# Float64 weights to float32: the low word added as an integer instead of multiplied and added as a float

## The chip, the core and the metric

The kernel runs on one core of a Trainium2 chip. The time is device microseconds (us) of one execution; lower is better. The engines named below are TensorE (PE; its weight loads are PEld), VectorE (DVE), ScalarE (ACT), GpSimd (POOL) and the queue that issues the transfers (SP). Each engine takes its own instructions strictly in the order in which they stand in its queue.

## What is computed

Causal attention over 4 batches of 8 heads with 576 tokens of 64 features, mixed with a linear-attention memory by a gate, gives 2304 rows of 512 numbers. These go through two gated feed-forward blocks:

```python
gate = 1.0 / (1.0 + np.exp(-(x @ w_gate)))     # 512 x 1536
val = x @ w_val                                # 512 x 1536
x = (gate * val @ w_out).astype(np.float32)    # 1536 x 512
h = x @ w_in                                   # 512 x 2048
g = h * np.clip(h + 3.0, 0.0, 6.0) / 6.0
return (g @ w_out).astype(np.float32)          # 2048 x 512
```

The five weight matrices arrive as float64. The kernel gets their bits as pairs of 32-bit words, a low and a high word for each number, makes float32 of them, and splits each float32 in an upper and a lower part for TensorE, so that every product is three matrix multiplications (upper by upper, upper by lower, lower by upper).

## The kernel before

Three phases share the engines. **Phase A** (to about 395 us) runs the attention, in 32 visits of one head pair and one half of its rows, and mixes into it the first half (6 of 12 column blocks of 128) of the first feed-forward block for the first 1872 tokens, in six chunks of 312 (`moe_a`). **Phase B** (to about 684 us) does the rest of the first block: 36 items of one token chunk and one column block each, `g1` (two products into `g`, then the tanh of line 673 on ACT, the multiplication of line 674 on DVE, and the split of the result `hs` on ACT and DVE) and, one item later, `g2` (the product of `hs` into `acc`). **Phase C** does the second block in three groups of 768 tokens, with seven products for the eight of a 2 by 2 block multiplication (`product`, line 787) and the product of the gated result into `acc` (line 822).

The weights of phases A and B and those of C are converted while A and B run. `w_load` fetches two tiles of 512 columns a time, as 128 x 512 pairs of words, into one of two buffers `wst`; `w_convert` turns the older buffer into float32 through `value`, which works in a scratch tile `wf` with a single buffer. In phase A one conversion takes both tiles at once (`self.wide` is 2: 9 conversions of 1024 columns); after that it takes one tile (`self.wide` is 1: 50 conversions of 512 columns, 18 for phase B and 32 for phase C). `convert` adds the upper part (ACT, line 163) and the lower part (DVE, line 164) and writes them to `wslot`; `convert_pair` does so for phase C, where 16 of the 32 tiles first go through four sums (lines 184 to 187) and are then split (lines 201 and 202), and stores the result in DRAM (`wd`).

In phase B a call of `w_next` (convert one pair of tiles, load the next) stands behind an item by the count in `goal`:

```python
goal = min(2 * i + 2, 4) + (max(i - 1, 0) * 2 * NPAIR + 26) // 27
while done < min(goal, 4 + 2 * NPAIR):
    self.w_next()
```

With NPAIR = 8 the last of the 20 calls is written behind the 28th of the 36 items. Behind the 31st and 32nd item stand `c_load(0)` and `c_sums()`: phase C's first input `xh` is loaded, its second half into a buffer `wst` once that is free, the other `wst` becomes `xt`, and POOL forms three sums in them (line 735). Behind the 32nd to 35th item stand 2, 2, 1 and 2 of the seven `c_block` calls, each of which splits one block of 768 columns (`xq`) on ACT and DVE (lines 228 and 229).

That is the order in which the code is written. On TensorE phases A and C keep it. Everywhere else a scheduler sets the order of each queue when the program is built, from its own estimate of every instruction's time: an instruction that it expects to be late is put behind others.

Of the kernel before, what the change touches and what calls it, by code (L numbers as in the profile page):

```python
# [8 lines left out]
F32 = mybir.dt.float32  # L9
F32R = mybir.dt.float32r  # L10
I32 = mybir.dt.int32
U32 = mybir.dt.uint32
AF = mybir.ActivationFunctionType
ALU = mybir.AluOpType
# [64 lines left out]
class Kernel:  # L79
# [64 lines left out]

    def value(self, st):

        nc = self.nc
        lo, hi = st[:, :, :, 0], st[:, :, :, 1]
        w = self.stage.tile([128, self.wide, 512], F32, name="wf", tag="wf", bufs=1)
        wi, hif, lof = w.bitcast(I32), hi.bitcast(F32), lo.bitcast(F32)  # L150
        nc.scalar.activation(w, hif, AF.Abs)
        nc.vector.tensor_scalar(w, w, HI_MIN, HI_MAX, op0=ALU.max, op1=ALU.min)
        nc.vector.tensor_scalar(wi, wi, 0x07FFFFFF, 3, op0=ALU.bitwise_and, op1=ALU.logical_shift_left)
        nc.vector.scalar_tensor_tensor(hi, hi, -0x40000000, wi, op0=ALU.bitwise_and, op1=ALU.bitwise_or)
        nc.vector.tensor_scalar(wi, hi, -0x800000, None, op0=ALU.bitwise_and)
        yield hif
        nc.vector.scalar_tensor_tensor(lof, lo.bitcast(U32), 2.0**-52, w, op0=ALU.mult, op1=ALU.mult)
        nc.vector.tensor_tensor(hif, hif, lof, op=ALU.add)

    def convert(self, sl, st):  # L160
        nc = self.nc
        for hif in self.value(st):
            nc.scalar.copy(sl[:, 0], hif)
        nc.vector.tensor_tensor(sl[:, 1], hif, sl[:, 0].bitcast(F32), op=ALU.subtract)

    def convert_pair(self, j, up, st):
# [807 lines left out]
```

## Time and profile before

| | |
|---|---|
| median of 3 runs | 1079.51 us (1079.44 to 1081.23) |
| the profiled execution | 1079.94 us |
| its span, first to last instruction | 1078.2 us |
| TensorE busy | 1037.6 us (96%), 5824 matmuls |
| VectorE busy | 684.2 us (63%), 1602 instructions |
| ScalarE busy | 551.5 us (51%), 1191 instructions |
| GpSimd busy | 83.2 us (8%), 102 instructions |
| 16 DMA engines busy | 44.5% of the span |

The profile is of one execution. A busy TensorE is not one at its peak, since matmuls overlap; what matters is where it has no matmul at all, and at which clock it works. The granted clock is a share of 2.4 GHz; 0.5 is 1.2 GHz, and a value between them is a mean over a stretch in which both occurred.

### The profile page before, as it was taken

To read this page: it belongs to the slowest core of one execution; us is meant where nothing else is said; L and a number is where in the kernel's file an instruction comes from. 1 tells how busy PE (TensorE), PEld (TensorE's weight loads), DVE (VectorE), ACT (ScalarE), POOL (GpSimd) and SP (SyncE) were. 2 spreads that over 40 slices of the span, in tenths; PEclk is the share of its full clock that TensorE was granted. 3 is DMA by queue.
4 is the path that set the end of the run, shared out by engine and by line. 5 is a ranking of instruction groups with operands and counts; after the bars stand their busy time and mean duration, and the time that the engine had idled before them with its cause. 6 is when DMAs were issued, how large, how long until landed. Compare 5 with 4: busy or idle time off the path is not lost.

```text
span 1078.2 us, 16086 instructions
## 1 busy us (share of the span) xinstructions
PE 1037.6 (96%) x5824; PEld 890.3 (83%) x5824; DVE 684.2 (63%) x1602; ACT 551.5 (51%) x1191; POOL 83.2 (8%) x102
## 2 busy tenths in 40 slices
PE   4789999999999999999999999799999999999998
PEld 2457768877887899999888888688888888888886
DVE  7999885454455348899898988854355333643432
ACT  5989885576556644435434433434344333543432
POOL 3212211110111000000000000320002000000000
PEclk9879999999999999999999999899999999999999
DMA  6645642424242225227586776645305543044511
GB/s 217 220 170 182 202 129 68 141 79 120 59 134 79 64 85 175 93 102 260 216 292 221 257 250 221 228 178 215 122 27 184 186 148 135 1 153 190 215 40 59
DMA packets 66239, 164.87 MB, mean 153 GB/s; under 512 B 8432, under 2 KB 41712, under 8 KB 60272
## 3 DMA queue, kind: packets, MB, share of 16 engines
q1 hardware_dynamic: 66160, 163.85, 44.5%
q8 instruction: 46, 0.75, 0.3%
q14 instruction: 33, 0.27, 0.1%
HBM read 122.76 MB, written 41.06 MB: 152 GB/s over the span
## 4 chain that ended last, share of the span: by engine, by line
PE 85%; DVE 7%; ACT 3%; DMA 2%; issue 1%; POOL 1%; SPq 0%; POOLq 0%; ACTq 0%
PE acc L822 18%; PE pa L787 9%; PE pb L787 7%; PE g L235 6%; PE g L233 6%; PE g L234 6%; PE m L233 5%; PE m L234 5%; PE m L235 5%; PE pv L426 4%; PE t L402 4%; PE s L344 3%; PE acc L233 3%; PE acc L235 3%; PE acc L234 3%; DMA aux<-in_aux 2%
## 5 line engine op out<-in xcount | busy, mean ns | idle before, releaser
L822 PE MATMUL acc<-wslot,hs 128*128 128x512 f32 x864 | 227.8, 395 | 2.2 <-ACT hs L228 2.2
L822 PEld LDWEIGHTS acc<-wslot,hs 128*128 128x128 f32 x864 | 159.5, 188 | 27.7 <-ACT hs L228 3.5
L787 PE MATMUL pa<-xq,wslot 128*128 128x384 f32 x576 | 119.3, 342 | 7.3 <-ACT xq L228 5.4
L787 PEld LDWEIGHTS pa<-xq,wslot 128*128 128x128 f32 x576 | 105.1, 190 | 16.6 <-ACT xq L228 5.8
L235 PE MATMUL g<-xs,wslot 128*128 128x468 f32 (+1 forms) x288 | 106.1, 369 | 0.0
L234 PE MATMUL g<-xs,wslot 128*128 128x468 f32 (+1 forms) x288 | 105.6, 369 | 0.0
L233 PE MATMUL g<-xs,wslot 128*128 128x468 f32 (+1 forms) x288 | 103.9, 369 | 0.0
L362 ACT ACTIVATE P<-P,m 128x192 f32<-128x192 f32 (+4 forms) x144 | 84.1, 586 | 31.2 <-DVE m L324 29.8
L233 PE MATMUL m<-xs,wslot 128*128 128x312 f32 x288 | 93.7, 325 | 0.0
L787 PE MATMUL pb<-xq,wslot 128*128 128x384 f32 x432 | 89.1, 341 | 0.2 <-DVE xq L229 0.2
L234 PE MATMUL m<-xs,wslot 128*128 128x312 f32 x288 | 88.1, 306 | 0.0
L235 PE MATMUL m<-xs,wslot 128*128 128x312 f32 x288 | 87.8, 305 | 0.0
L344 PE MATMUL s<-qk 64*128 64x320 f32 (+3 forms) x320 | 70.8, 502 | 14.3 <-DMA qk<-in_qk 11.8
L787 PEld LDWEIGHTS pb<-xq,wslot 128*128 128x128 f32 x432 | 78.6, 189 | 7.0 <-DVE xq L229 0.7
L851 DVE TENSOR_TENSOR c<-pb,u 128x384 f32<-128x384 f32 x48 | 26.6, 555 | 88.1 <-ACT u L887 87.1
L402 PEld LDWEIGHTS t<-ident,P 128*128 128x128 f32 x464 | 53.8, 145 | 27.2 <-issue 14.5
L799 ACT ACTIVATE r<-c,three 128x384 f32<-128x384 f32 x72 | 44.2, 614 | 61.9 <-DVE c L851 61.9
L402 PE MATMUL t<-ident,P 128*128 128x128 f32 x464 | 68.4, 285 | 7.5 <-POOL P L377 4.1
L229 DVE TENSOR_TENSOR hs<-r,hs 128x384 fp32r<-128x384 f32 x96 | 55.9, 586 | 26.3 <-ACT hs L228 24.8
L404 ACT COPY T<-t 128x512 f32<-128x512 f32 (+2 forms) x128 | 65.7, 540 | 12.1 <-PE t L402 11.9
L324 DVE CUSTOM_DVE_ANT_0 P<-s,mask 128x320 f32<-128x320 f32 (+3 forms) x144 | 62.5, 451 | 14.5 <-PE s L344 14.2
L426 PE MATMUL pv<-T,aux 128*64 128x256 f32 (+2 forms) x512 | 63.4, 377 | 4.5 <-ACT T L404 4.5
(102 smaller groups left out, 1966.9 us busy)
## 6 DMA issues: line engine op xcount, KB each, us to landing
wst<-in_wm SPq DMA_DIRECT2D x68, 512.0 KB, 5.7
wslot<-wd SPq DMA_DIRECT2D x30, 1024.0 KB, 5.0
wd<-wslot SPq DMA_DIRECT2D x16, 1024.0 KB, 4.4
wslot<-wd SPq DMA_DIRECT2D x15, 768.0 KB, 6.3
wd<-wslot SPq DMA_DIRECT2D x8, 768.0 KB, 5.8
qk<-in_qk SPq DMA_DIRECT2D x32, 160.0 KB, 2.3
aux<-in_aux SPq DMA_DIRECT2D x16, 320.0 KB, 3.3
qk<-in_qk SPq DMA_DIRECT2D x16, 288.0 KB, 3.0
```

The source lines that it names most:

```text
L229: elo.tensor_tensor(lo, src, hi.bitcast(F32), op=ALU.subtract)
L233: nc.tensor.matmul(out, w[0], x[0], start=first, stop=False)
L234: nc.tensor.matmul(out, w[0], x[1], start=False, stop=False)
L235: nc.tensor.matmul(out, w[1], x[0], start=False, stop=last)
L324: self.nc.vector.tensor_tensor_reduce(out=self.row(v, rg, r, 64 + a, 64 + e), in0=ps, in1=mask, scale=-0.125, scalar=3.0e38 if a == 0 else ...
L344: nc.tensor.matmul(ps[:, : e - a], qk[rows, 0, q0 : q0 + 128], qk[rows, 1, a:e], start=True, stop=True)
L362: self.nc.scalar.activation(x, x, AF.Exp, bias=vs["m", rg][:, r : r + 1], scale=-1.0, accum_out=vs["l", rg][:, r : r + 1])
L402: nc.tensor.transpose(ps[:, 128 * n : 128 * n + 128], self.row(v, rg, r, 128 * j, 128 * j + 128), self.ident)
L404: nc.scalar.copy(pr["T", rg][:, 512 * k : 512 * k + c], ps[:, :c])
L426: nc.tensor.matmul(ps[rows, o : o + w], pr["v"][:, j, rows], T[:, c : c + w], start=(n == 0), stop=(n == last), skip_group_check=True,)
L787: nc.tensor.matmul(ps[:, :HC], w[:, i, b, cc], x[:, l, k], start=first and k == 0 and n == 0, stop=last and k == 1 and n == 2, skip_group_ ...
L822: nc.tensor.matmul(a, h[:, i, cc], w[:, l, f], start=first and f == 0 and n == 0, stop=last and f == 1 and n == 2)
```

## The change

`value` keeps its first four steps: the absolute value of the high word read as a float (ACT), clamp, mask and shift, and the joining of sign and shifted bits (DVE). After these the high word holds a float32 whose last three bits are open; the low word's top bits belong there. Before, the exponent of that float was masked out into `wf` (line 155), the low word as an integer was multiplied with 2^-52 and that power of two (line 157), and the product was added as a float (line 158). Now the low word is scaled by 2^-29 and rounded to an integer, and the two words are added as integers: the last bits of the float are counted up. In conversions of one tile the scaling is done on ACT, into the low word's place, and the join goes to `wf`, from which `convert` takes the upper part; in conversions of two tiles the scaling is done on DVE into `wf`.

```diff
-        wi, hif, lof = w.bitcast(I32), hi.bitcast(F32), lo.bitcast(F32)
+        wi, hif = w.bitcast(I32), hi.bitcast(F32)
         nc.scalar.activation(w, hif, AF.Abs)
         nc.vector.tensor_scalar(w, w, HI_MIN, HI_MAX, op0=ALU.max, op1=ALU.min)
         nc.vector.tensor_scalar(wi, wi, 0x07FFFFFF, 3, op0=ALU.bitwise_and, op1=ALU.logical_shift_left)
+        if self.wide == 1:
+            nc.scalar.activation(lo, lo.bitcast(U32), AF.Copy, scale=2.0**-29)
+            nc.vector.scalar_tensor_tensor(wi, hi, -0x40000000, wi, op0=ALU.bitwise_and, op1=ALU.bitwise_or)
+            yield w
+            nc.vector.tensor_tensor(hi, wi, lo, op=ALU.add)
+            return
         nc.vector.scalar_tensor_tensor(hi, hi, -0x40000000, wi, op0=ALU.bitwise_and, op1=ALU.bitwise_or)
-        nc.vector.tensor_scalar(wi, hi, -0x800000, None, op0=ALU.bitwise_and)
         yield hif
-        nc.vector.scalar_tensor_tensor(lof, lo.bitcast(U32), 2.0**-52, w, op0=ALU.mult, op1=ALU.mult)
-        nc.vector.tensor_tensor(hif, hif, lof, op=ALU.add)
+        nc.vector.tensor_scalar(wi, lo.bitcast(U32), 2.0**-29, None, op0=ALU.mult)
+        nc.vector.tensor_tensor(hi, hi, wi, op=ALU.add)
...
-        for hif in self.value(st):
-            nc.scalar.copy(sl[:, 0], hif)
+        hif = st[:, :, :, 1].bitcast(F32)
+        for upper in self.value(st):
+            nc.scalar.copy(sl[:, 0], upper)
```

In the built program lines behind the change stand 7 lower: line 164 is now 171, 229 is 236, 674 is 681. The integer addition (line 159, or 164 for two tiles) becomes an instruction that the listing calls ISA, with 512 (1024) times 2 elements in a lane.

The scheduler builds other queues from it. At the end of phase B, VectorE's queue before, from the 36th and last item's line 674 on (`wst` and `wf` are the conversion, `hs` the item, `xp` phase B's output):

```order
L674 SCALAR_TENSOR_TENSOR th<-th,g 128x468
L152 TENSOR_SCALAR wf<-wf 128x512
L164 TENSOR_TENSOR wslot<-wst,wslot 128x512
L153 TENSOR_SCALAR wf<-wf 128x512
L229 TENSOR_TENSOR hs<-th,hs 128x468
L154 SCALAR_TENSOR_TENSOR wst<-wst,wf 128x512
L155 TENSOR_SCALAR wf<-wst 128x512
L157 SCALAR_TENSOR_TENSOR wst<-wst,wf 128x512
L158 TENSOR_TENSOR wst<-wst 128x512
L694 SCALAR_TENSOR_TENSOR xp<-acc,xp 128x468 x2
L164 TENSOR_TENSOR wslot<-wst,wslot 128x512
```

The last conversion stands behind the last item there. VectorE's queue now, from just ahead of the 32nd item's line 681 to just behind the 34th's:

```order
L157 SCALAR_TENSOR_TENSOR wf<-wst,wf 128x512
L681 SCALAR_TENSOR_TENSOR th<-th,g 128x468
L159 ISA wst<-wst,wf 128x512x2
L236 TENSOR_TENSOR xq<-xh,xq 128x768
L171 TENSOR_TENSOR wslot<-wst,wslot 128x512
L236 TENSOR_TENSOR hs<-th,hs 128x468
L681 SCALAR_TENSOR_TENSOR th<-th,g 128x468
L236 TENSOR_TENSOR xq<-xt,xq 128x768
L236 TENSOR_TENSOR hs<-th,hs 128x468
L236 TENSOR_TENSOR xq<-xh,xq 128x768
L681 SCALAR_TENSOR_TENSOR th<-th,g 128x468
L236 TENSOR_TENSOR xq<-xt,xq 128x768
```

The last conversion ends (line 171) between the 32nd and the 33rd item, and the splits of phase C's first blocks (`xq`), of which five stood behind the last item, all stand ahead of it.

ScalarE's queue in phase B before, from the 30th item's tanh on:

```order
L673 ACTIVATE th<-g 128x468
L228 CAST xs_6906<-x 128x468
L151 ACTIVATE wf<-wst 128x512
L228 CAST xs_6909<-x 128x468
L228 CAST xs_6912<-x 128x468
L228 CAST xs_6915<-x 128x468
L228 CAST hs<-th 128x468
L151 ACTIVATE wf<-wst 128x512
```

ScalarE's queue now at the same item (line 156 is the new scaling of the low word, 152 the absolute value):

```order
L680 ACTIVATE th<-g 128x468
L156 ACTIVATE wst<-wst 128x512
L235 CAST xs_6847<-x 128x468
L235 CAST xs_6850<-x 128x468
L235 CAST xs_6853<-x 128x468
L156 ACTIVATE wst<-wst 128x512
L152 ACTIVATE wf<-wst 128x512
L235 CAST xs_6856<-x 128x468
L235 CAST hs<-th 128x468
```

Two scalings now stand ahead of the cast of `hs`, each of which needs a weight tile that has landed.

In phase A the fifth conversion's second half stood so in VectorE's queue (line 324 is the attention's row maximum, two rows each; 297 and 299 prepare the next visit):

```order
L155 TENSOR_SCALAR wf<-wst 128x1024
L157 SCALAR_TENSOR_TENSOR wst<-wst,wf 128x1024
L324 ISA P,m<-s,mask 128x320
L324 ISA m 128x1
L324 ISA P,m<-s,mask 128x320
L324 ISA m 128x1
L297 TENSOR_SCALAR phw<-aux 128x256
L158 TENSOR_TENSOR wst<-wst 128x1024
```

and now so:

```order
L163 TENSOR_SCALAR wf<-wst 128x1024
L306 SCALAR_TENSOR_TENSOR ph<-aux,phw 128x256
L331 ISA P,m<-s,mask,m 128x256
L331 ISA m 128x1
L495 SCALAR_TENSOR_TENSOR th<-th,m 128x312
L331 ISA P,m<-s,mask 128x192
L331 ISA m 128x1
L164 ISA wst<-wst,wf 128x1024x2
```

One instruction of the conversion is gone, and the attention's stand closer together.

## Rows read from the trace of the kernel before

**Rows 1.** Busy time by stretch: from:to, length, PE, PEld, DVE, ACT, POOL (instructions), PEclk, DMA share, GB/s

```profile
13.00:66.00 53.00, 40.81 (x212) 23.70 (x214) 52.07 (x146) 48.06 (x118) 11.74 (x14) 0.84 0.59 189
66.00:95.00 29.00, 26.89 (x198) 21.15 (x195) 26.75 (x68) 25.51 (x59) 4.95 (x6) 1.00 0.60 200
95.00:160.00 65.00, 63.20 (x426) 46.98 (x424) 57.09 (x171) 56.07 (x143) 14.07 (x18) 1.00 0.55 168
...
440.00:676.00 236.00, 236.00 (x1135) 212.66 (x1134) 211.75 (x397) 100.24 (x169) 0.00 (x0) 1.00 0.60 214
676.00:700.00 24.00, 16.49 (x69) 14.25 (x68) 19.30 (x27) 8.68 (x16) 8.19 (x4) 0.79 0.69 243
```

**Rows 2.** Timeline of PE, end of phase B: start, length, engine, line, tiles, count [idle before]

```profile
683.51 0.38 PE L235 MATMUL acc<-hs,wslot 128*128 128x468 f32 x1
689.27 0.69 PE L787 MATMUL pa<-xq,wslot 128*128 128x384 f32 x1 [5.38 <-ACT xq L228]
691.30 1.97 PE L787 MATMUL pa<-xq,wslot 128*128 128x384 f32 x5 [1.34 <-DVE xq L229]
...
697.97 1.33 PE L787 MATMUL pa<-xq,wslot 128*128 128x384 f32 x6 [0.57 <-ACT u L887]
699.13 1.22 PE L787 MATMUL pb<-xq,wslot 128*128 128x384 f32 x6
...
704.63 1.22 PE L787 MATMUL pa<-xq,wslot 128*128 128x384 f32 x6
705.69 1.32 PE L822 MATMUL acc<-wslot,hs 128*128 128x512 f32 x5
```

**Rows 3.** Timeline of DVE (32nd, 33rd and 36th item, last conversion) and POOL

```profile
646.26 0.64 DVE L674 SCALAR_TENSOR_TENSOR th<-th,g 128x468 f32<-128x468 f32 x1 [0.24 <-PE g L235]
...
653.80 0.64 DVE L674 SCALAR_TENSOR_TENSOR th<-th,g 128x468 f32<-128x468 f32 x1 [0.59 <-PE g L235]
...
676.87 0.63 DVE L674 SCALAR_TENSOR_TENSOR th<-th,g 128x468 f32<-128x468 f32 x1
...
683.76 0.68 DVE L164 TENSOR_TENSOR wslot<-wst,wslot 128x512 fp32r<-128x512 f32 x1
...
684.67 1.81 POOL L735 TENSOR_TENSOR xt<-xh 128x768 f32<-128x768 f32 x1 [319.82 <-DVE wslot L164]
...
688.31 2.12 POOL L735 TENSOR_TENSOR xh<-xh 128x768 f32<-128x768 f32 x1
```

**Rows 4.** Groups by line and shape: tiles, count, then busy us, mean ns, idle before

```profile
L157 DVE SCALAR_TENSOR_TENSOR wst<-wst,wf 128x512 f32<-128x512 uint32 x50 | 34.6, 692 | 1.2
L158 DVE TENSOR_TENSOR wst<-wst 128x512 f32<-128x512 f32 x50 | 34.4, 691 | 6.1 <-ACT wslot L163 3.8
L151 ACT ACTIVATE wf<-wst 128x512 f32<-128x512 f32 x50 | 34.0, 679 | 32.9 <-DVE wst L157 24.1 <-DMA wst<-in_wm 7.1 <-DVE wst L158 1.7
L155 DVE TENSOR_SCALAR wf<-wst 128x512 int32<-128x512 int32 x50 | 21.5, 431 | 1.0
L158 DVE TENSOR_TENSOR wst<-wst 128x1024 f32<-128x1024 f32 x9 | 11.8, 1315 | 0.1
L157 DVE SCALAR_TENSOR_TENSOR wst<-wst,wf 128x1024 f32<-128x1024 uint32 x9 | 11.0, 1225 | 0.0
L155 DVE TENSOR_SCALAR wf<-wst 128x1024 int32<-128x1024 int32 x9 | 6.6, 735 | 0.0
```

**Rows 5.** Busy time by stretch of line 154 alone, once in each conversion

```profile
440.00:676.00 236.00, 26.18 (x38) 1.00 0.60 214
```

**Rows 6.** Timeline of phase A: the fourth conversion's end on DVE, SP's next transfers

```profile
65.37 1.22 DVE L164 TENSOR_TENSOR wslot<-wst,wslot 128x1024 fp32r<-128x1024 f32 x1
...
66.61 0.80 SPq L142 DMA_DIRECT2D wst<-in_wm  x2
67.51 0.38 SPq L272 DMA_DIRECT2D aux<-in_aux  x1
```

**Rows 7.** The chain that ended last, 67 to 73 us: start, length, what

```profile
67.51 5.09 DMA aux<-in_aux
```

**Rows 8.** Waits: who waited for whom, us in total, times, longest

```profile
ACT wf L151 <- DMA wst<-in_wm: 10.3, 7, 2.7
```

## The prediction

> **What bounds the kernel now.** I read the busy time by stretch first, since the shares over the whole span mix stages with different limits. In phase B, from 440 to 676 us, TensorE is busy for all of the 236 us [rows 1] while VectorE is busy for 211.75: nothing that VectorE saves there can shorten that stretch itself. Two other places are open. From 13 to 66 us [rows 1] VectorE is busy 52.07 of 53 us, ScalarE 48.06, and TensorE only 40.81, at a mean granted clock of 0.84: here VectorE's queue, with ScalarE's close behind, sets the pace. After that TensorE fills up: it lacks 2.1 us from 66 to 95 and 1.8 from 95 to 160. The other place is the seam between B and C: from 676 to 700 us [rows 1] TensorE is busy 16.49 of 24 us and the clock is 0.79.
>
> The timelines show why. TensorE's last matmul of phase B starts at 683.51; the next, of phase C, waits 5.38 us for a block `xq`, and the stretch only runs evenly again from 699.13 [rows 2]. `xq` waits for POOL's sums, and the first of these starts at 684.67, released by line 164 of the last conversion, which ends at 684.4 [rows 3]. That is a wait for a buffer: `xt` takes a `wst` buffer that the last weight tile held. The last conversion was written behind the 28th item but ran behind the 36th. VectorE at 90% in phase B costs no time there and pushes the conversions, in small steps, behind the end of the phase. That lateness is paid once, at the seam.
>
> **The change, conversions of one tile.** Line 155 (431 ns), 157 (692) and 158 (691), together 1.814 us of VectorE, give way to one integer addition [rows 4]. The trace of before has no such instruction. The nearest row is line 158, which adds the same 512 words in the same buffers in 0.69 us. The built program gives 1024 elements in a lane, halves of words; if those went one by one the row is line 158 with 1024 elements, 1.315 us. I take 0.8, near the first, since the words are the same, and keep 0.69 and 1.32 as ends. So a conversion loses 1.0 us of VectorE (0.5 to 1.1).
>
> The Trainium skill, "VectorE: DVE Perf Modes", speaks against a plain form of this addition (Specifications): VectorE computes in FP32, and integers are exact only below 2^24, which a float's bit pattern is not. That fits an instruction on halves, and the same page (the perf-mode tier table) lets a two-input operation on 16-bit data take two elements a cycle where 32-bit data takes one. By that the addition would be an estimate of 0.69 us and the saving 1.1; without the double rate it is 1.32 and 0.5. No row of before shows 16-bit operands on VectorE.
>
> In phase B 38 conversions run between 440 and 676 us [rows 5], so VectorE falls from 211.75 by 38 x 1.0 = 38 (19 to 42) to some 174 us of 236 (170 to 193), 74%. In none of these cases is it full. ScalarE gains the scaling, priced by line 151, which reads the same strided words, at 0.68 us [rows 4]: 38 x 0.68 = 26 us on top of 100.24 of 236 [rows 1], so 53%. TensorE's own work hides that, as long as the scaling doesn't wait (the slower rival, below).
>
> **The seam.** In the new queue the last conversion ends between line 674 of the 32nd and of the 33rd item (681 there). Before, these ran at 646.26 and 653.80 [rows 3], and the items are paced by TensorE, which stays full. So `wst` is free at about 653 instead of 684.4. POOL's three sums took from 684.67 to 690.43 [rows 3], 5.8 us: they end near 660, some 24 us ahead of the end of phase B, and the seven `xq` are split between the remaining items, where the new queue has them. Now the price: from the last matmul of B, which issues for about 0.21 us from 683.51, to the even run at 699.13 are 15.4 us. In them TensorE does 24 matmuls of 384 columns (groups of 1, 5, 1, 5, 6 and 6, of which the first two and the last stand in [rows 2]). At full clock six of them take 705.69 - 704.63 = 1.06 us [rows 2], so 24 take 4.2. What is lost is 11.2 us: the wait of 5.38, smaller ones, and matmuls at the lower clock level, since 5 of them took 1.97 us at 691.30 right behind the wait [rows 2]. Something stays late after the change: the product waits for ScalarE's copies of its own partial result (0.57 us at 697.97 [rows 2]), and with nothing to fill in at the first step of phase C that happens twice. I leave 1.2 us for it. **Seam: -10 us** (-7 if the blocks come only partly in time, -11.2 if nothing stays).
>
> **The change, conversions of two tiles.** Lines 155, 157 and 158 with 1024 elements take 735 + 1225 + 1315 = 3.275 us [rows 4]. In their place stand a scaling that reads strided words and writes dense ones with one input, as line 155 does (0.735; 1.225 if it behaves as line 157), and the addition (1.315 to 2.63, twice line 158; I take 1.5 as above). The saving is 3.275 - 2.235 = 1.04 us (from 1.2 down to a loss of 0.6). Four conversions end by 66.6 us [rows 6], so 4.2 us leave a VectorE queue that is 98% full. That queue holds the chain up in two ways: the attention's instructions are queued behind the conversion's, and the transfers are queued behind it too. At 65.37 the fourth conversion's last step ran; it frees `wst`, only then SP issues the weight transfer at 66.61, and the attention's `aux` stands behind that at 67.51 [rows 6] and is on the chain of waits for 5.09 us [rows 7]. But ScalarE at 48.06 of 53 us lies close behind and loses nothing by wide conversions. I count two thirds, 2.8 us, and nothing for the 5 conversions behind. **Phase A: -3 us.** Ends: all nine and part of the low clock of 13 to 66 us back, -8; the dear ends of both prices, 9 x 0.6 = 5 us more on VectorE, +5.
>
> **Sum.** The profiled execution took 1079.94 us: 1079.94 - 10 - 3 = 1066.9. It lies 0.4 above the median, so the forecast for the median is 1066.5. Phase C is left alone.
>
> **Rivals.**
> 1. *Only the seam is gained.* In phase A the scheduler has reordered VectorE's queue and SP's transfers, and ScalarE, nearly full, takes over as the bound. Then 1079.5 - 10 = 1069.5, and up to 1075 with phase A's dear end. For it: ScalarE's 91% from 13 to 66 us. Against: VectorE is fuller, and several of TensorE's waits there end with it.
> 2. *The change does not relieve VectorE*: the addition costs what it replaces, the conversions run as late as before, the seam stays, 1079 (within 0.2%). It decides at 1.81 us for 512 words, above both bounds; and the queue, which is fixed when the program is built, already has the conversions ahead. Nothing in the rows speaks for it.
> 3. *Slower: the scaling blocks ScalarE.* Two scalings now stand ahead of the cast of `hs` in ScalarE's queue, and each needs a tile that has landed. If the transfer is later than the scheduler thought, tanh and cast stand behind it, then VectorE, then `g2` on TensorE. Before, line 151 had the same wait, 7 times, 10.3 us, 2.7 at most [rows 8], and TensorE in phase B lost nothing. `hs` is needed one item later, so that a wait decides only when it is longer than most of an item, which takes 653.80 - 646.26 = 7.5 us. If each of the 25 loads after phase A overran that slack by 0.7 us, 17.5 us would go on TensorE: 1066.5 + 17.5 = 1084.
> 4. *Better*: phase A gives 8: 1061.5.
>
> **How the numbers follow.** Forecast as summed 0.60, only the seam 0.22, no relief 0.07, ScalarE blocked 0.05, better 0.06. A run can tell 0.2%, 2.2 us, from no change. Faster: 0.60 + 0.22 + 0.06 = 0.88; same 0.07; slower 0.05. The range from 1061 (seam -10, phase A -8) to 1075 (seam -10, phase A +5; or seam -7 with phase A +2) leaves out rivals 2 and 3 and a little of each end.
>
> **What would show it.** Right: the first of POOL's sums starts about 30 us earlier relative to phase B's last matmul; between that matmul and the first of line 822 (now 829) no wait over 1 us and a granted clock of 1.00; VectorE busy near 74% in phase B, ScalarE near 53%, TensorE still full; the addition near 0.8 us, its wide form near 1.5; TensorE's idle time from 13 to 66 us smaller by about 3. Wrong: a seam that still waits for `xq` (then the sums, the load of `xh` or SP's order are late next), TensorE waiting for `hs` in phase B (rival 3), or phase A with more idle time than before.

## The result and the profile after

| | before | after |
|---|---|---|
| median | 1080.37 us (1079.44 to 1082.49) | 1070.11 us (1067.11 to 1071.72) |
| ratio, 95% interval | | 0.9899 (0.9869 to 0.9929) |
| the profiled execution | 1079.94 us | 1071.72 us |
| its span | 1078.2 us | 1069.9 us |
| VectorE busy | 684.2 us | 623.7 us |
| ScalarE busy | 551.5 us | 576.6 us |

The change gains 10.3 us at the median; 13.0 were forecast (1079.51 to 1066.5). The profiled execution of after is the longest of its group; a second profile of the same kernel took 1069.12 us, and both are used below.

The busy time by stretch answers to [rows 1]; the columns are those given there.

```profile
13.00:66.00 53.00, 42.83 (x244) 26.42 (x244) 48.14 (x146) 48.01 (x119) 12.73 (x15) 0.90 0.63 196
66.00:95.00 29.00, 25.33 (x167) 19.85 (x165) 23.33 (x62) 25.90 (x60) 4.25 (x5) 0.88 0.56 187
95.00:160.00 65.00, 62.26 (x417) 46.32 (x416) 46.83 (x151) 54.96 (x139) 13.59 (x17) 0.97 0.53 165
...
440.00:676.00 236.00, 236.00 (x1134) 212.69 (x1133) 186.12 (x336) 125.10 (x216) 8.22 (x4) 1.00 0.64 233
676.00:700.00 24.00, 22.93 (x117) 20.73 (x117) 12.62 (x20) 8.20 (x17) 5.51 (x3) 1.00 0.53 183
```

Three things are to be seen. From 676 to 700 us TensorE is busy 22.93 us in place of 16.49, at full clock. In phase B VectorE falls by 25.6 us and ScalarE rises by 24.9, while TensorE stays full: there alone nothing would be gained. From 13 to 66 us VectorE is no longer full, and TensorE is busy 2.0 us longer, at a granted clock of 0.90 in place of 0.84. But it is busy 1.6 us less from 66 to 95 and 0.9 less from 95 to 160, and its clock there is 0.88 and 0.97 where it was 1.00 before. What phase A gains early, it loses again behind.

TensorE at the seam, from phase B's last matmul on, answers to [rows 2]:

```profile
684.89 0.38 PE L242 MATMUL acc<-hs,wslot 128*128 128x468 f32 x1
685.11 1.21 PE L794 MATMUL pa<-xq,wslot 128*128 128x384 f32 x6
...
687.87 1.31 PE L794 MATMUL pa<-xq,wslot 128*128 128x384 f32 x6 [0.50 <-ACT u L884]
689.75 1.33 PE L794 MATMUL pa<-xq,wslot 128*128 128x384 f32 x6 [0.57 <-ACT u L894]
690.91 1.22 PE L794 MATMUL pb<-xq,wslot 128*128 128x384 f32 x6
```

The even run begins 690.91 - 684.89 = 6.0 us behind phase B's last matmul; before it was 699.13 - 683.51 = 15.6. No wait for `xq` is left, only the two for ScalarE's copies that the prediction had left 1.2 us for (0.50 + 0.57). POOL's first and third sum, which answer to [rows 3]:

```profile
650.52 2.05 POOL L742 TENSOR_TENSOR xt<-xh 128x768 f32<-128x768 f32 x1 [284.31 <-DMA x<-xp]
...
654.44 1.85 POOL L742 TENSOR_TENSOR xh<-xh 128x768 f32<-128x768 f32 x1
```

They start 34.4 us ahead of phase B's last matmul instead of 1.2 behind it. The row names a transfer as what released the first sum, but the last conversion (line 171) had ended only 0.2 us before, at 650.30. The groups of the changed lines answer to [rows 4] (159 and 164 are the integer addition, 163 and 156 the scaling for two tiles and for one):

```profile
L159 DVE CUSTOM_DVE_ANT_0 wst<-wst,wf 128x1024 uint16<-128x1024 uint16 x50 | 34.6, 692 | 1.6
L164 DVE CUSTOM_DVE_ANT_0 wst<-wst,wf 128x2048 uint16<-128x2048 uint16 x9 | 11.5, 1280 | 0.0
L163 DVE TENSOR_SCALAR wf<-wst 128x1024 int32<-128x1024 uint32 x9 | 6.2, 685 | 0.0
L156 ACT ACTIVATE wst<-wst 128x512 int32<-128x512 uint32 x50 | 33.8, 679 | 11.3 <-DMA wst<-in_wm 11.1
```

The addition takes 692 ns for 512 words, the low end of the prediction's bounds, and 1280 ns for 1024. The rows count 1024 elements of 16 bits where line 158 before had 512 of 32 bits in 691 ns. With the estimate of 0.69 us that the prediction made from the Trainium skill, "VectorE: DVE Perf Modes", for an addition at the double rate, the trace agrees. At which rate the engine worked no run shows, only the time.

### The profile page after: what moved, and what is told of

It reads as the page before. It is cut to its first block, busy times and chain, and to the rows that moved or that the text cites. A ratio compares the mean times of both kernels' runs of the same rounds, so it can differ in the third digit from the quotient of the medians.

```text
span 1069.9 us, 15995 instructions
## 1 busy us (share of the span) xinstructions
PE 1035.4 (97%) x5824; PEld 890.1 (83%) x5824; DVE 623.7 (58%) x1493; ACT 576.6 (54%) x1241; POOL 83.3 (8%) x102
## 4 chain that ended last, share of the span: by engine, by line
PE 88%; DMA 4%; ACT 3%; DVE 3%; issue 1%; SPq 1%; POOL 0%; ACTq 0%; DVEq 0%
PE acc L829 18%; PE pa L794 9%; PE pb L794 7%; PE m L240 6%; PE g L242 6%; PE g L240 6%; PE g L241 6%; PE m L241 5%; PE m L242 5%; PE pv L433 4%; PE t L409 4%; PE s L351 4%; PE acc L240 3%; PE acc L241 3%; PE acc L242 3%; DMA aux<-in_aux 1%
## 5 line engine op out<-in xcount | busy, mean ns | idle before, releaser
L829 PEld LDWEIGHTS acc<-wslot,hs 128*128 128x128 f32 x864 | 159.5, 188 | 27.7 <-ACT hs L235 3.5
L240 PE MATMUL m<-xs,wslot 128*128 128x312 f32 x288 | 94.8, 329 | 1.9 <-DVE m L331 1.9
L241 PE MATMUL m<-xs,wslot 128*128 128x312 f32 x288 | 89.2, 310 | 0.0
L242 PE MATMUL m<-xs,wslot 128*128 128x312 f32 x288 | 89.0, 309 | 0.0
```

The lines of the kernel that those rows point to most:

```text
L240: nc.tensor.matmul(out, w[0], x[0], start=first, stop=False)
L241: nc.tensor.matmul(out, w[0], x[1], start=False, stop=False)
L242: nc.tensor.matmul(out, w[1], x[0], start=False, stop=last)
L829: nc.tensor.matmul(a, h[:, i, cc], w[:, l, f], start=first and f == 0 and n == 0, stop=last and f == 1 and n == 2)
```

## Experiments

The times of before beside each are of the same chip as the kernel that it is compared with: 1080.63 us for the first four, 1080.03 for the next four, 1081.08 for the last two.

### Two tiles only, one tile only

The first keeps the new code for conversions of two tiles and the old code for those of one:

```diff
-            nc.scalar.activation(lo, lo.bitcast(U32), AF.Copy, scale=2.0**-29)
...
-            nc.vector.tensor_tensor(hi, wi, lo, op=ALU.add)
+            nc.vector.tensor_scalar(wi, hi, -0x800000, None, op0=ALU.bitwise_and)
...
+            nc.vector.scalar_tensor_tensor(lof, lo.bitcast(U32), 2.0**-52, w, op0=ALU.mult, op1=ALU.mult)
+            nc.vector.tensor_tensor(hif, hif, lof, op=ALU.add)
```

> Only the conversions of two tiles are changed; those of one tile are as before. Theory: the gain of 10 us comes from the seam between phases B and C alone, and that from the conversions of one tile, because VectorE is full in phase B. So the seam stays as before (some 15 us between phase B's last matmul and the even run of phase C, with POOL's first sum released by the last conversion), and phase A gains 0 to 3 us: 1077 to 1080. Rival (phase A is where VectorE's time counts, the seam is a by-product): 1072 or less.

The second does the reverse:

```diff
-        nc.vector.tensor_scalar(wi, lo.bitcast(U32), 2.0**-29, None, op0=ALU.mult)
-        nc.vector.tensor_tensor(hi, hi, wi, op=ALU.add)
+        lof = lo.bitcast(F32)
+        nc.vector.scalar_tensor_tensor(lof, lo.bitcast(U32), 2.0**-52, w, op0=ALU.mult, op1=ALU.mult)
+        nc.vector.tensor_tensor(hif, hif, lof, op=ALU.add)
```

> Only the conversions of one tile are changed; those of two tiles, in phase A, are as before. Theory: the seam falls from 15.6 to 6 us as in the changed kernel, so that nearly all of the gain is here: 1070 to 1073. In phase A VectorE is as full as before, and scalings of the low word stand in ScalarE's queue near 130 us, ahead of the attention's copies, so TensorE's idle time there is 1 to 3 us more than before. Rival: 1077 or more, if both halves of the change are needed for the seam.

| | median | ratio, 95% interval | against before |
|---|---|---|---|
| two tiles only | 1077.66 us | 0.9969 (0.9954 to 0.9984) | -3.0 us |
| one tile only | 1072.96 us | 0.9937 (0.9923 to 0.9950) | -7.7 us |

Both fell where expected, and their sum, -10.7, is the whole gain. Which part does what is read from TensorE's timeline at the seam. Two tiles only:

```profile
681.39 0.38 PE L244 MATMUL acc<-hs,wslot 128*128 128x468 f32 x1
...
687.81 0.69 PE L796 MATMUL pa<-xq,wslot 128*128 128x384 f32 x1 [6.04 <-ACT xq L237]
...
697.64 1.20 PE L796 MATMUL pb<-xq,wslot 128*128 128x384 f32 x6
```

One tile only:

```profile
685.72 0.38 PE L244 MATMUL acc<-hs,wslot 128*128 128x468 f32 x1
...
688.70 1.31 PE L796 MATMUL pa<-xq,wslot 128*128 128x384 f32 x6 [0.50 <-ACT u L886]
690.58 1.33 PE L796 MATMUL pa<-xq,wslot 128*128 128x384 f32 x6 [0.57 <-ACT u L896]
691.74 1.22 PE L796 MATMUL pb<-xq,wslot 128*128 128x384 f32 x6
```

With two tiles only the seam stays (16.3 us) and phase B ends 2.1 us earlier than before; with one tile only the seam is gone (6.0 us, a gain of 9.6) and phase B ends 2.2 us later. So the new conversions of one tile are the whole of the seam's gain.

### More work on VectorE, in steps

To see whether relief of VectorE closes the seam, the changed kernel got its clamp one, two or three times over in each conversion of one tile, which changes no value and costs 0.43 us a time.

```diff
         nc.vector.tensor_scalar(w, w, HI_MIN, HI_MAX, op0=ALU.max, op1=ALU.min)
+        for _ in range(3 if self.wide == 1 else 0):
+            nc.vector.tensor_scalar(w, w, HI_MIN, HI_MAX, op0=ALU.max, op1=ALU.min)
```

> The changed kernel once more, beside the three others of this group. Theory: 1067 to 1072 us, as in its first runs, and the time follows the granted clock of phase A (lower clock, longer time): phase B and the seam alike in each execution.

> The changed kernel with three more clamps on VectorE in each conversion of one tile (the clamp repeated, which changes no value), so that VectorE carries some 1.28 us more in each of 50 conversions and is about full again in phase B. Theory (the seam is paid because VectorE cannot get the conversions done before phase B ends): the last conversion again ends behind the last item, the seam costs about 15 us again from phase B's last matmul to the even run, 1078 to 1081 us. Rival (the seam went because the code is new, or because ScalarE scales the low word): the seam stays at 6 us and the time at 1068 to 1072.

> The changed kernel with one more clamp (the clamp repeated, which changes no value) in each conversion of one tile: +0.43 us each, some 17 us in the 38 conversions of phase B, so VectorE would carry 203 of 236 us. In the queue the last conversion ends behind the 34th item. Theory (only VectorE's overflow past the end of phase B is paid): POOL's sums start about 15 us later than in the changed kernel, still ahead of the end of phase B, the seam stays near 6 us, 1069 to 1073 us. Rival (each us more on VectorE costs its share, so that padding acts in proportion: three pads cost 39 us): 1081 to 1084 us.

> The same with two more clamps: +0.85 us in each conversion, 32 us in phase B, VectorE would carry 218 of 236 us, a little more than before (212), and in the queue the last two conversions end behind the last item. Theory (only the overflow is paid): the first of POOL's sums falls behind phase B's last matmul, the seam costs 15 to 25 us in place of 6, 1078 to 1088 us. Rival (in proportion): 1094 to 1097 us.

| clamps added | median | first sum, against phase B's last matmul | seam | VectorE, 440 to 676 us |
|---|---|---|---|---|
| 0 | 1069.12 us | 647.91 - 682.29 = -34.4 | 6.0 us | 184.29 us |
| 1 | 1070.94 us | 671.85 - 684.71 = -12.9 | 6.0 us | 198.83 us |
| 2 | 1090.83 us | 694.85 - 682.29 = +12.6 | 27.0 us | 203.58 us |
| 3 | 1108.57 us | 713.72 - 677.06 = +36.7 | 51.0 us | 205.30 us |
| (kernel before) | 1080.03 us | 684.67 - 683.51 = +1.2 | 15.6 us | 211.75 us |

The kernels with 0 and 3 clamps ran on one chip, those with 1 and 2 on another, where before took 1081.08 us; costs below are taken against the before of the same chip. TensorE in the kernel with one clamp more:

```profile
684.71 0.37 PE L244 MATMUL acc<-hs,wslot 128*128 128x468 f32 x1
...
689.57 1.31 PE L796 MATMUL pa<-xq,wslot 128*128 128x384 f32 x6 [0.57 <-ACT u L896]
690.72 1.20 PE L796 MATMUL pb<-xq,wslot 128*128 128x384 f32 x6
```

and with two:

```profile
682.29 0.38 PE L244 MATMUL acc<-hs,wslot 128*128 128x468 f32 x1
...
699.45 0.69 PE L796 MATMUL pa<-xq,wslot 128*128 128x384 f32 x1 [16.78 <-ACT xq L237]
...
709.28 1.20 PE L796 MATMUL pb<-xq,wslot 128*128 128x384 f32 x6
```

The first clamp costs 0.8 us, which is within the spread of the runs, the second 20 us, the third 19. What is paid is only what runs over the end of phase B: in the three kernels whose sums come late the seam is 14.4 us plus the lateness (before 1.2 + 14.4 = 15.6; 12.6 + 14.4 = 27.0; 36.7 + 14.4 = 51.1). With three clamps the seam grows by 24 us and the time by 19 only, because phase B ends 5.2 us earlier there than with two (677.06 and 682.29); that comes from phase A, below. The rival that every us on VectorE costs its share, 1081 to 1084 with one clamp, is refuted.

With three clamps the expectation of 1078 to 1081 was 28 us too low, since I had VectorE's load at about that of before and took the lateness to be the same. With two it missed too, by 3 us above its range. With one clamp the time came as expected, but the sums started 21.5 us later than in the changed kernel, not 15. The table's last column shows why load misleads: two clamps leave VectorE less busy (203.58) than before (211.75), and yet the conversions end 11 us later. VectorE's groups from 395 to 720 us in that kernel (busy us, mean ns, idle before):

```profile
L173 DVE TENSOR_TENSOR wslot<-wst,wslot 128x512 fp32r<-128x512 f32 x34 | 23.5, 691 | 14.2 <-ACT wslot L172 12.7
...
L153 DVE TENSOR_SCALAR wf<-wf 128x512 f32<-128x512 f32 x49 | 20.8, 425 | 10.8 <-ACT wf L152 10.6
```

It waits 23.3 us for ScalarE there. The same two steps before (lines 164 and 152) waited almost nothing and 4.2 us. The transfers of the weights, which need a free `wst`, come late as well: with three clamps ScalarE's scaling waits 41.4 us for them from 395 to 720 us, where it waits 11.1 in the whole span of after. A reading of the code, which no run isolates: three VectorE instructions used to stand between the upper part's copy and its use, now one does, and ScalarE has one step more in each conversion, in front of a scratch tile that exists once. What decides is when the chain of a conversion ends, not one engine's share.

### The conversions written earlier, in the kernel before

```diff
-            goal = min(2 * i + 2, 4) + (max(i - 1, 0) * 2 * NPAIR + 26) // 27
+            goal = min(2 * i + 2, 4) + (max(i - 1, 0) * 2 * NPAIR + 22) // 23
```

> The kernel before, with the calls that convert phase C's weights written earlier in phase B (the last of them behind the 24th instead of the 28th item). Theory (VectorE's throughput sets when the last conversion ends, not the place where it is written): the seam and the time stay as before, 1078 to 1082 us. Rival (the place in the program set the lateness): the seam shrinks to about 6 us, 1068 to 1072 us.

1079.91 us, ratio 1.0 (0.9989 to 1.0011). POOL and TensorE:

```profile
686.83 1.80 POOL L735 TENSOR_TENSOR xt<-xh 128x768 f32<-128x768 f32 x1 [319.82 <-DVE wslot L164]
```

```profile
685.68 0.38 PE L235 MATMUL acc<-hs,wslot 128*128 128x468 f32 x1
...
691.43 0.69 PE L787 MATMUL pa<-xq,wslot 128*128 128x384 f32 x1 [5.38 <-ACT xq L228]
...
701.59 1.21 PE L787 MATMUL pb<-xq,wslot 128*128 128x384 f32 x6
```

The sum again starts 1.2 us behind phase B and still waits for the last conversion (line 164). The traces show why: the instructions of VectorE, ScalarE, GpSimd and SP run one by one in the same order as before. The scheduler undid the edit, and this run is the kernel before once more. It shows that the place in the code doesn't set the place in the queue, and the rival falls in that form. Whether another order would have had the conversions done sooner stays open: before, VectorE was idle for 24 of the 236 us from 440 to 676 (line 674 waits 14.1 us for TensorE's `g` from 395 to 700), with the rest of its queue standing behind.

### The scaling on VectorE, everywhere or until phase B

```diff
-            nc.scalar.activation(lo, lo.bitcast(U32), AF.Copy, scale=2.0**-29)
+            nc.vector.tensor_scalar(lo, lo.bitcast(U32), 2.0**-29, None, op0=ALU.mult)
```

> As the changed kernel, but VectorE scales the low word in conversions of one tile too; ScalarE gets no new work. Theory: VectorE's relief in a conversion is then about 0.69 us in place of 1.12, still enough that the conversions are not late, so the seam is as in the changed kernel; and the 2 to 3 us that TensorE waits near 130 to 140 us for the attention's copies behind the scalings on ScalarE are gone: 1066 to 1069, 1 to 3 us below the changed kernel. Rival: those waits have another cause (the changed order of phase A), and the time is that of the changed kernel, 1070; or VectorE is full again and the seam comes back, 1077.

Until phase B, with a flag that `phase_b` sets:

```diff
-            nc.scalar.activation(lo, lo.bitcast(U32), AF.Copy, scale=2.0**-29)
+            if self.scale_act:
+                nc.scalar.activation(lo, lo.bitcast(U32), AF.Copy, scale=2.0**-29)
+            else:
+                nc.vector.tensor_scalar(lo, lo.bitcast(U32), 2.0**-29, None, op0=ALU.mult)
```

> As the changed kernel, but the conversions of one tile that are written ahead of phase B have their low word scaled on VectorE, the later ones on ScalarE. Theory: no scaling stands in ScalarE's queue while the attention runs, TensorE's waits near 130 to 140 us go, phase B is as in the changed kernel: 1066 to 1069. Rival, as for the run with all scalings on VectorE: 1070.

Everywhere: 1069.78 us (1066.74 to 1070.24), ratio 0.9901 (0.9887 to 0.9915). Until phase B: 1070.39 us (1068.84 to 1072.68), ratio 0.9915 (0.9901 to 0.9930). Neither can be told from the changed kernel's 1069.12 and 1070.11: the gain that was expected of them isn't there. With the scaling on VectorE everywhere, that engine carries 195.41 us of phase B and ScalarE 104.74, and the seam still closes, since the first sum starts 24 us ahead of phase B's end:

```profile
658.50 1.85 POOL L742 TENSOR_TENSOR xt<-xh 128x768 f32<-128x768 f32 x1 [294.74 <-DMA xh<-x]
```

So the seam's gain comes from two instructions in place of three: here 0.42 us for the scaling and 0.69 for the addition, where 1.81 stood before. The move to ScalarE is not needed for it.

### The scaling of two tiles on GpSimd

```diff
-        nc.vector.tensor_scalar(wi, lo.bitcast(U32), 2.0**-29, None, op0=ALU.mult)
+        nc.gpsimd.tensor_scalar(wi, lo.bitcast(U32), 2.0**-29, None, op0=ALU.mult)
```

> The changed kernel with the scaling of the nine two-tile conversions on GpSimd instead of VectorE: 9 x 0.685 = 6 us less on VectorE in phase A. If VectorE still bounds phase A: 3 to 5 us faster than the changed kernel, 1065 to 1067. If ScalarE, the transfers or the clock bound it now: the same, 1069 to 1072. If GpSimd needs far longer than 0.7 us for it, the conversions end later: 1072 to 1078.

1084.44 us, ratio 1.0045 (1.0029 to 1.0061): slower even than before, and beyond the dearest case expected. The line on GpSimd (duration ns min/median/max), and what TensorE then waits for:

```profile
L163 POOL TENSOR_SCALAR wf<-wst x9: 2851/2877/2974, 17.9 to 123.0; 128x1024 int32<-128x1024 uint32 x9
```

```profile
118.17 0.41 PE L242 MATMUL m<-ha,wslot 128*128 128x312 f32 x1 [2.27 <-DVE wslot L171]
...
123.51 0.63 PE L240 MATMUL m<-ha,wslot 128*128 128x312 f32 x1 [4.18 <-ACT wslot L170]
...
129.34 0.63 PE L242 MATMUL m<-ha,wslot 128*128 128x312 f32 x1 [4.94 <-DVE wslot L171]
```

The scaling takes 2.88 us there and 0.685 on VectorE. The last conversions of two tiles come too late for the first block's weights, and TensorE stands still for 11.4 us in these three waits. Because the conversions were delayed as well, this run doesn't answer whether VectorE's load alone still bounds phase A.

### Phase A, place by place

TensorE works through the 32 visits of phase A in one order in all kernels, so the start of a visit's first `pv` product can be compared between traces. Start less that of before, in us (visits 5, 7, 12, 13 and 32 start at 62.93, 88.82, 133.62, 148.94 and 390.75 us before):

| kernel | 5 | 7 | 12 | 13 | 32 | clock, 66 to 95 us | clock, 95 to 160 us |
|---|---|---|---|---|---|---|---|
| (kernel before) | 0 | 0 | 0 | 0 | 0 | 1.00 | 1.00 |
| after | -3.3 | -0.1 | -0.7 | +1.3 | +1.4 | 0.88 | 0.97 |
| after, second profile | -5.1 | -3.1 | -2.9 | -0.6 | -1.2 | 0.88 | 0.97 |
| one clamp more | -3.5 | -2.3 | -2.8 | +0.7 | +0.7 | 0.94 | 0.95 |
| two clamps more | -4.8 | -3.3 | -3.3 | -1.1 | -1.1 | 0.88 | 0.97 |
| three clamps more | -4.9 | -4.9 | -5.7 | -6.6 | -6.4 | 1.00 | 1.00 |
| two tiles only | -3.3 | -1.2 | -2.1 | -1.5 | -2.1 | 0.88 | 1.00 |
| scaling on VectorE | -3.4 | -1.5 | -0.6 | -1.0 | -1.1 | 0.94 | 1.00 |
| on VectorE until phase B | -5.4 | -3.4 | -2.6 | -2.6 | -2.6 | 0.88 | 1.00 |
| one tile only | 0.0 | +1.5 | +0.7 | +2.1 | +2.2 | 0.94 | 0.97 |
| before, written earlier | -1.1 | +2.1 | +1.5 | +2.4 | +2.2 | 0.94 | 1.00 |

The last row has the same queues as before, and still differs by up to 2.4 us: that is how far one profile can be read. Beyond it stands the lead at the fifth visit, 3.3 to 5.4 us in all eight profiles with the new conversion of two tiles on VectorE. By the seventh visit 1.1 to 3.2 of it are gone in seven of them, and in these the granted clock fell for some us between 66 and 95 us. With three clamps, in its one profile, it stayed at 1.00 there and nothing is gone. TensorE's wait for VectorE's row maximum `m` near 68 us, in after:

```profile
68.88 1.11 PE L351 MATMUL s<-qk 64*128 64x256 f32 x4 [1.82 <-DVE m L331]
```

With three clamps the same wait is 1.70 us. Why the clock falls behind the one and not behind the other no run isolates.

From the 12th to the 13th visit the five profiles with a clock of 0.97 or 0.95 lose 1.4 to 3.5 us, most in the one with 0.95. A clock of 0.97 over 65 us stands for 2.0 us less at full speed, 0.95 for 3.3 (an estimate from the table); what counts is a few us at 0.50 right behind a wait. All five scale on ScalarE in phase A, but so does the kernel with three clamps, which gains 0.9 there at 1.00; the other four without a fall lose 0.9 at most. What TensorE waits for in this place is the last copy to `T`. Before, and in after:

```profile
135.56 0.86 PE L426 MATMUL pv<-T,aux 128*64 128x256 f32 x6 [0.76 <-ACT T L404]
136.83 0.86 PE L433 MATMUL pv<-T,aux 128*64 128x256 f32 x6 [2.07 <-ACT T L411]
```

ScalarE's queue before, where the copy (line 404) stands ahead of four multiplications of the attention's rows (line 390), and in after, where it (411) stands behind them (397):

```profile
135.04 0.47 ACT L404 COPY T<-t 128x384 f32<-128x384 f32 x1
135.40 2.57 ACT L390 ACTIVATE P<-P,l 128x448 f32<-128x448 f32 x4
```

```profile
133.85 2.56 ACT L397 ACTIVATE P<-P,l 128x448 f32<-128x448 f32 x4
136.31 0.46 ACT L411 COPY T<-t 128x384 f32<-128x384 f32 x1
```

The longer wait goes with the scheduler's new order. With three clamps the copy stands ahead as before, and the wait is 0.27 us. All other kernels with new code have it behind, "two tiles only" (a wait of 1.85 us) and the two that scale on VectorE (1.46 and 1.49) too, so the scalings on ScalarE aren't needed for the order. In the five profiles that have both, the wait is 2.06 to 2.72 us and the clock falls behind it; whether the scalings cause that no run isolates.

The two profiles of after differ as was expected of the second: phase B's last matmul stands 2.6 us apart, the spans too (1069.9 and 1067.3 us), and the granted clock from 13 to 66 us is 0.90 and 0.97.

## Why the prediction came out as it did

The median, 1070.11, lies 3.6 us above the forecast of 1066.5 and inside the range. Step by step:

- **The seam: right.** -10 forecast, 9.6 measured. The place, the wait (a buffer that the last conversion held), its release some 30 us earlier (34.4 against phase B's end) and what stays late (0.50 and 0.57 us) are as written. The clamps show the mechanism, and that the gain has an edge: lateness is paid from the end of phase B on and at no earlier point. That VectorE, busy for 90% of phase B, had pushed the last conversion behind the 36th item, as the prediction has it, is not shown: the scheduler had put it there when the program was built.
- **The addition: right, at its low end.** 0.8 taken, 0.692 measured; for two tiles 1.5 taken, 1.280 measured, and 0.685 instead of 0.735 for the scaling. A conversion of two tiles saves 3.275 - 1.965 = 1.31 us, where 1.04 was counted, so the size of the phase A term was not missed on the instructions.
- **Phase A: the mis-sized term.** -3 forecast; in the two profiles of after the last visit starts 1.4 later and 1.2 us earlier, and the medians leave 10.3 - 9.6 = 0.7 us for it. The relief of VectorE was there, and larger than the 2.8 us counted for the first four conversions: 3.3 and 5.1 us at the fifth visit. What the sum left out is what came behind: it took ScalarE's queue and the clock of 1.00 from 66 us on as they were. The new order put a copy that TensorE needs behind 2.56 us of other work, and the granted clock fell at both places where the lead is lost. With three clamps neither happened in those places, and the last visit started 6.4 us early, near the forecast's better end of -8. Alone, conversions of two tiles gained 3.0; conversions of one tile gained 7.7 where the seam alone is 9.6, so they give back 1.9. What sets off the clock's fall stays open; moving the scaling off ScalarE gained nothing that can be measured.
- **Rival 1, only the seam**, with 1069.5, is thus nearest to the time. Its reason holds in part: the scheduler's new order did cost TensorE a wait, in ScalarE's queue. But phase A's lead was won first and lost later, at a lower clock, which the rival doesn't name.
- **Rival 2** is refuted by 692 ns and by the seam. **Rival 3**, ScalarE blocked in phase B, did not occur: ScalarE did wait longer for transfers, as feared, but TensorE stays full at 236.00 us. The waits, of the whole span, that answer to [rows 8]:

```profile
ACT wf L152 <- DMA wst<-in_wm: 17.5, 8, 3.8
ACT wst L156 <- DMA wst<-in_wm: 11.1, 14, 2.4
```

  The longest, 3.8 us, is under the 7.5 us of an item from which the rival was to decide.
- **The shares in phase B.** ScalarE 53%, as forecast. VectorE 79% instead of 74%: 25.6 us fewer, not 38. From 440 to 676 us the three old instructions took 68.0 us and the addition takes 27.7, so the price was right; but five more splits `xq` (4.9 us), which stood behind phase B, and one to two more conversions now fall into the stretch. That cost nothing, and "VectorE is not full" was not quite the right test either, as the clamps show.

## What to carry to other kernels

Work that a full engine covers costs nothing until it runs over the end of that cover; then each us of lateness is paid in full. So ask when the last piece of it ends against the event that needs it, not how busy its engine is: here 13 us of slack were left with one clamp more, and one clamp further cost 20 us. Where a scheduler builds the queues, look up in the built queue what an edit has moved, on every engine: one edit here moved nothing, and another moved a copy that TensorE needed. And read the granted clock beside each gain, for a lead can be lost to it.

## What the hardware showed unexpectedly

- An addition of 512 words as 1024 elements of 16 bits takes 692 ns on VectorE, what the float addition of the same 512 words took (691).
- The scaling of 1024 strided words takes 685 ns on VectorE, less than the masking of 1024 such words before (735), and 2877 on GpSimd.
- Two profiles of one and the same order of phase A ended 2.2 us apart, and the changed kernel's runs went from 1067.11 (granted clock 0.995) to 1071.72 (0.990): differences of that size can't be read from single profiles.
- Behind waits of TensorE of much the same length the granted clock fell in some profiles and not in others: from 66 to 95 us it was 0.88 in after, 1.00 with three clamps (waits of 1.82 and 1.70 us), and the last visit of phase A started 7.8 us apart.
